# Results written over their own input tile: no result buffers, 14 places for the transposed input, a new order

## The chip, the cores and the metric

One core of one Trainium2 chip. The metric is the device time of one execution in microseconds (us). The kernel before took 220.41 us, the median of three runs (220.10 to 221.13).

## What is computed

Four batches of 12,480 rows x of width 128, 32 inducing rows, and a two-layer block with a hidden width of 2,048, all float32:

```
def mab(q, kv):
    s = scale * (q @ kv.transpose(0, 2, 1))
    s = s - s.max(-1, keepdims=True)
    a = np.exp(s)
    a /= a.sum(-1, keepdims=True) + 1e-09
    return a @ kv
h = mab(I, x)                  # I: the 32 inducing rows, for each batch
x2 = mab(x, h)                 # each row of x attends to the 32 rows of h
hid = x2 @ w_in
return (hid - np.tanh(hid)) @ w_out
```

## The kernel before

A batch b goes through three parts. `first` is mab(I, x): for each of seven tiles s (six of 1,920 rows, the last, "xl", of 960) TensorE makes scores from the transposed tile xT and the inducing rows (L322), VectorE copies them and takes maxima (L348), ScalarE takes exponentials (L398), VectorE transposes them (L402), and TensorE sums them with the tile xn, the same rows in natural layout, over the whole batch into one PSUM bank (L409). xn is loaded from a second copy in memory (L391), or, for the eight tiles listed in `TURNED`, made on the chip from xT with TensorE transposes (L381, L387). `SPLIT` cuts a batch's tiles into two groups with a maximum of each. At the end the matrix hT of the batch is written (L468, L470).

`linear` folds the two-layer block into a 32 x 128 matrix P4 for the batch (L491 to L551). This works while the hidden values are so small, or so alike over the 32 rows, that a bound holds; `bound` evaluates it (L672 to L711), writes `limit`, and a general path that isn't taken here follows.

`second` is mab(x, h) with P4 in place of h, tile by tile (`b_chain`): scores with hT on the same xT tile (L322), VectorE transposes and takes maxima (L594, L596), GpSimd subtracts (L601), ScalarE exponentiates (L603), GpSimd adds two halves into a tile bs (L608), VectorE sums (L611) and inverts (L614), GpSimd scales (L615), VectorE transposes (L618), TensorE multiplies with P4 (L643) into two PSUM tiles of a pool with two places, ScalarE (in the last batch also VectorE) evicts each into half a tile of 960 columns (L649), and SP stores it (L653).

So an xT tile is loaded once and used by `first` and later by `second`. Buffers come from pools whose sizes are in `PLACES`: ten places for xT, five for xn (which also hold the raw weights, L277, while they are converted, L281 to L302), five for the result halves `ot`, ten bs tiles. In the last batch two results share a free xT place instead.

All loads and stores are issued by SP, in one queue. The order on every engine is made when the program is built: each operation has a cost and a priority, mostly a sum of numbers of `ORD`, and `Plan.order` lets each engine start the ready operation with the lowest priority whose buffers are free. Engines then execute in that fixed order, each waiting for what it needs. Into planned gaps of TensorE, as far as `FILL` allows, matmuls without use are put (L734).

Of the kernel before, what the change touches and what calls it, by code (L numbers as in the profile page):

```python
# [20 lines left out]
SEG = 480  # L21
KB = SEG // 32
NT = 4
SG = NQ * SEG
SMALL = 0.0625
SERIES = (1.0 / 3.0, -2.0 / 15.0, 17.0 / 315.0)
ROUND = 2.0 ** -24
FILL = 0.5
PLACES = dict(xT=10, xn=5, s1=1, be=5, bt=3, et=3, ot=5, ps=3, o=2, bs=10, D=1, M4=1, P1=2, P4=2)

ORD = dict(first=(-45, 295, 470, 815), second=(630, 840, 935, 580), fs=15, ss=23, lx=-271, ln=-96, lns=3, turn=61,
           keep=0, q=-129, half=-504, late=51, guard=859, win=-335, wout=-461, lwin=-435.5, lwout=32.5, store=-199,
           base=8)
TURNED = {(0, 0), (0, 1), (0, 2), (0, 4), (1, 5), (2, 2), (2, 5), (3, 3)}

SPLIT = {1: 5, 2: 4, 3: 5}
IN_LAG, OUT_LAG = 3, 1.7
SLACK = 1.0e-3

POLY = (0.333333333, -0.133333309, 0.0539675967, -0.0218625754, 0.00882625035,  # L40
# [24 lines left out]
class Plan:  # L65
# [5 lines left out]
    def add(self, eng, cost, fn, reads=(), writes=(), pri=0.0, lag=0.15, turn=None, other=None):  # L71

        deps = set()
        for x in reads:
            if x.writer:
                deps.add(x.writer)
        for x in writes:
            if x.writer:
                deps.add(x.writer)
            deps.update(x.readers)  # L80
        op = Op(eng, cost, fn, deps, list(dict.fromkeys([*reads, *writes])), pri, lag + (0.1 if eng == "PE" else 0.0))
        op.turn, op.other = turn, other
        for x in reads:
            x.readers.append(op)
        for x in writes:
            x.writer, x.readers = op, []
        for x in op.bufs:
            x.left += 1
        self.ops.append(op)
        return op  # L90
# [90 lines left out]
def fused_kernel(ctx, tc, xT, xn, xl, indT, w_in, w_out, outT):  # L181
    nc = tc.nc
    C, NTOK = xT.shape
    B = xn.shape[0]
# [27 lines left out]

    plan = Plan(PLACES)
    add = plan.add

    def io_buf(tag, shape):
        return Buf(lambda: io.tile(shape, F32, name=tag, bufs=PLACES[tag]), tag)

    def small(name, shape, bufs=2):
        return Buf(lambda: io.tile(shape, F32, name=name, bufs=bufs))  # L220

    def misc():
        return Buf(lambda: ps_m.tile([128, 512], F32, name="ps_m"), "ps")
# [9 lines left out]
    sums_all = small("S_all", [128, B * NSG * KB], 1)  # L233
    bs_tiles = [io.tile([128, KB, m // 2 + 1], F32, name=f"bs_{k}", bufs=1) for k in range(PLACES["bs"])]
    bs_next = itertools.count()
# [83 lines left out]
    def scores(ps, rows, w):  # L319

        for q, row in enumerate(rows):
            nc.tensor.matmul(ps[q * m:(q + 1) * m, :SEG], lhsT=w, rhs=row, start=True, stop=True)  # L322

    def attend(b, pri, s1, group, nbs, sms, at, hacc):
# [9 lines left out]
        for s in group:  # L334
# [3 lines left out]
                out=x.get()[:, :nq * SEG], in_=xT[:, b * N + base:b * N + base + nq * SEG]),  # L338
                writes=[x], pri=pri + s - ORD["lx"], lag=IN_LAG, turn="xT")
            ps = misc()  # L340

            def pe(x=x, ps=ps, nq=nq):
                t = x.get()[:, :nq * SEG].rearrange("c (k q j) -> c k q j", k=KB, j=32)
                scores(ps.get(), [t[:, :, q, :] for q in range(nq)], indT_sb)
            add("PE", 0.96, pe, reads=[x, ind_b, s1], writes=[ps], pri=pri + ORD["fs"] * s)

            def out(ps=ps, s=s, P=nq * m):
                nc.vector.tensor_scalar(out=s1.get()[:P, s, :], in0=ps.get()[:P, :SEG], scalar1=1.0, scalar2=None,  # L348
                                        op0=ALU.mult, op1=ALU.max, accum_out=mxg.get()[:P, s:s + 1])
            add("DVE", 0.68, out, reads=[ps, s1], writes=[s1_part[s], mxg], pri=pri + ORD["fs"] * s)  # L350

        mx, mr, nb = small("mx", [128, 1], 4), small("mr", [1, m], 4), Buf(lambda: nbs.get()[:, at:at + 1])
        ps, ps2 = misc(), misc()
        p = pri + ORD["base"]
        add("DVE", 0.12, lambda: nc.vector.tensor_reduce(out=mx.get(), in_=mxg.get(), axis=AX.X, op=ALU.max),
# [13 lines left out]
        for s in group:  # L369
# [3 lines left out]
            parts = []  # L373
            if (b, s) in TURNED and nq == NQ:
                for k in range(0, KB, NT):
# [3 lines left out]
                    def turn(pt=pt, k=k, n=n, s=s):  # L379
                        for i in range(n):  # L380
                            nc.tensor.transpose(out=pt.get()[:, i * 128:(i + 1) * 128],  # L381
                                                in_=xT_b[b, s].get()[:, (k + i) * 128:(k + i + 1) * 128], identity=ident)
                    add("PE", 0.13 * n, turn, reads=[xT_b[b, s], x, ident_b], writes=[pt], pri=pri + ORD["fs"] * s + ORD["turn"],
                        turn=None if k else "xn")

                    def keep(pt=pt, k=k, n=n, x=x):
                        nc.scalar.copy(out=x.get()[:, k:k + n, :].rearrange("p k c -> p (k c)"), in_=pt.get()[:, :n * 128])  # L387
                    add("ACT", 0.15 + 0.11 * n, keep, reads=[pt, x], writes=[part], pri=pri + ORD["fs"] * s + ORD["keep"])
                    parts.append(part)
# [27 lines left out]
    def first(b, pri):  # L417
        s1 = io_buf("s1", [128, NSG, SEG])
        cut = SPLIT.get(b, 0) if SPLIT.get(b, 0) < NSG else 0
        groups = [range(0, cut), range(cut, NSG)] if cut else [range(NSG)]  # L420
# [201 lines left out]
    def second(b, s, pri):  # L622
        base, nq = SGS[s]
        x = xT_b[b, s]
        n = (b * NSG + s) * KB

        def out(bt, held):
            ots = []
            for h in range(nq // 2):
                if b < B - 1:  # L630
                    ots.append(io_buf("ot", [128, 2 * SEG]))
                else:
                    if h == 0:

                        wide = io_buf("xT", [C, SG])
                    ots.append(Buf(lambda wide=wide, h=h: wide.get()[:, 2 * h * SEG:2 * (h + 1) * SEG]))
            keep = [wide] if b == B - 1 else []
            tiles = [Buf(lambda: ps_o.tile([128, 2, 512], F32, name="o"), "o") for _ in range(nq // 2)]

            def pe(qs):  # L640
                for q in qs:
                    p = slice(q * m, (q + 1) * m)
                    nc.tensor.matmul(tiles[q // 2].get()[:, q % 2, :SEG], lhsT=P4_b[b].get()[p, :], rhs=bt.get()[p, :],  # L643
                                     start=True, stop=True)

            add("PE", 1.05, lambda: pe(range(nq)), reads=[bt, *held, P4_b[b]], writes=tiles, pri=pri)
            for h, (o, ot) in enumerate(zip(tiles, ots)):
                def ev(copy, o=o, ot=ot):
                    copy(out=ot.get().rearrange("p (q n) -> p q n", q=2), in_=o.get()[:, :, :SEG])  # L649
                add("ACT", 0.97, lambda ev=ev: ev(nc.scalar.copy), reads=[o, *keep], writes=[ot], pri=pri,  # L650
                    other=("DVE", 1.14, lambda ev=ev: ev(nc.vector.tensor_copy), pri + 1000) if b == B - 1 else None)
                at = b * N + base + 2 * h * SEG
                add("SP", 1.2, lambda ot=ot, at=at: nc.sync.dma_start(out=outT[:, at:at + 2 * SEG], in_=ot.get()),  # L653
                    reads=[ot, *keep], pri=pri - ORD["store"], lag=OUT_LAG)
        b_chain(b, nq, x, x.get, pri, lambda: sums_all.get()[:, n:n + KB], out, b == B - 1 and s % 2 == 1)


# [71 lines left out]
    for op in ops:  # L729


        if not any(a < op.start < z for a, z in quiet):
            for _ in range(int(FILL * gaps.get(op, 0.0) / 0.25)):
                nc.tensor.matmul(bank[:, 2 * C:2 * C + 128], lhsT=ident, rhs=ident, start=first_fill, stop=True,  # L734
# [105 lines left out]
```

## Time and profile before

| | |
|---|---|
| median of the runs | 220.41 us |
| profiled execution | 221.32 us, span 219.6 us, mean granted TensorE clock 0.911 |
| TensorE, VectorE, ScalarE, GpSimd busy | 178.1, 155.3, 116.8, 97.8 us |
| DMA | 73.03 MB on the data queue, 87.3% of 16 engines' span |
| read and written | 47.46 MB, 25.56 MB |

Busy shares are averages over stretches with different limits; the prediction reads them stretch by stretch. A DMA share near 1 means that all 16 engines had packets to move all the time. A line number is that of the kernel before; in the kernel after, lines from L640 on are eight lower, so that the output matmul is L635, the eviction L641 and the store L645.

### The profile page before, as it was taken

To read this page: it belongs to the slowest core of one execution; us is meant where nothing else is said; L and a number is where in the kernel's file an instruction comes from. 1 tells how busy PE (TensorE), PEld (TensorE's weight loads), DVE (VectorE), ACT (ScalarE), POOL (GpSimd) and SP (SyncE) were. 2 spreads that over 40 slices of the span, in tenths; PEclk is the share of its full clock that TensorE was granted. 3 is DMA by queue.
4 is the path that set the end of the run, shared out by engine and by line. 5 is a ranking of instruction groups with operands and counts; after the bars stand their busy time and mean duration, and the time that the engine had idled before them with its cause. 6 is when DMAs were issued, how large, how long until landed. Compare 5 with 4: busy or idle time off the path is not lost.

```text
span 219.6 us, 5239 instructions
## 1 busy us (share of the span) xinstructions
PE 178.1 (81%) x2015; PEld 92.7 (42%) x2015; DVE 155.3 (71%) x402; ACT 116.8 (53%) x229; POOL 97.8 (45%) x138
## 2 busy tenths in 40 slices
PE   7565589848968999995799985998997999799740
PEld 7542244744432467332226651334454434346310
DVE  5799986543697995667388953496979048888960
ACT  2426356930324999385178961367943836648310
POOL 1135414000299643339454641189334245989600
PEclk9979679999999999999699995799999559889995
DMA  5999998799999899999999999599999924609793
GB/s 170 414 417 357 322 405 323 268 292 344 417 421 417 262 416 363 423 405 427 416 411 323 336 419 420 192 358 421 361 381 353 378 113 179 237 36 372 286 400 125
DMA packets 15472, 73.44 MB, mean 334 GB/s; under 512 B 1872, under 2 KB 1872, under 8 KB 15440
## 3 DMA queue, kind: packets, MB, share of 16 engines
q1 hardware_dynamic: 15440, 73.03, 87.3%
q8 instruction: 18, 0.29, 0.5%
q14 instruction: 14, 0.11, 0.2%
HBM read 47.46 MB, written 25.56 MB: 333 GB/s over the span
## 4 chain that ended last, share of the span: by engine, by line
PE 46%; DMA 25%; DVE 12%; ACT 6%; POOL 4%; issue 2%; SPq 1%; ACTq 0%; POOLq 0%; DVEq 0%
PE ps_m L322 17%; DMA xT<-in_xT 14%; PE o L643 10%; PE bank L409 6%; PE ps_m L381 5%; DMA outT<-ot 4%; DMA xn<-in_xl 4%; DMA xn<-in_w_out 3%; PE ps_m L491 2%; ACT xn L387 2%; DVE xT L649 2%; ACT s L398 2%; DVE xn L292 1%; DVE xn L298 1%; PE ps_m L549 1%
## 5 line engine op out<-in xcount | busy, mean ns | idle before, releaser
L601 POOL TENSOR_TENSOR be<-be,bmx 128x480 f32<-128x480 f32 (+1 forms) x25 | 25.2, 1013 | 49.3 <-DVE bmx L596 42.6
L322 PE MATMUL ps_m<-xT,indT_sb 128*32 128x480 f32 x208 | 32.6, 667 | 17.8 <-DMA xT<-in_xT 11.5
L649 ACT COPY ot<-o 128x960 f32<-128x960 f32 x39 | 36.4, 959 | 14.7 <-DMA outT<-ot 7.9
L643 PE MATMUL o<-bt,P 32*128 32x480 f32 x184 | 31.9, 654 | 3.6 <-ACT ot L649 2.9
L615 POOL TENSOR_TENSOR be<-be,brs 128x480 f32<-128x480 f32 (+1 forms) x25 | 24.8, 995 | 21.6 <-DVE brs L614 15.3
L409 PE MATMUL bank<-xn,et 128*32 128x128 f32 (+1 forms) x840 | 30.9, 280 | 4.3 <-DMA xn<-in_xn 2.9
L348 DVE TENSOR_SCALAR_CACHE_REDUCE s<-ps_m 128x480 f32<-128x480 f32 (+1 forms) x28 | 18.2, 650 | 20.4 <-PE ps_m L322 20.4
L409 PEld LDWEIGHTS bank<-xn,et 128*32 128x32 f32 (+1 forms) x840 | 23.8, 111 | 14.5 <-issue 5.9
L322 PE MATMUL ps_m<-xT,hT 128*32 128x480 f32 x208 | 28.0, 604 | 0.2 <-ACT D L507 0.2
L387 ACT COPY xn<-ps_m 128x512 f32<-128x512 f32 (+1 forms) x32 | 17.3, 556 | 11.6 <-PE ps_m L381 11.5
L608 POOL TENSOR_TENSOR bs<-be 128x240 f32<-128x240 f32 (+1 forms) x25 | 17.9, 718 | 10.5 <-ACT be L603 10.4
L734 PE MATMUL bank<-ident 128*128 128x128 f32 x110 | 20.2, 328 | 1.9 <-POOL ident masks.py:199 1.4
L402 DVE STREAM_TRANSPOSE et<-s 128x480 f32<-128x480 f32 (+1 forms) x28 | 18.4, 659 | 3.8 <-ACT s L398 3.8
L594 DVE STREAM_TRANSPOSE be<-ps_m 128x480 f32<-128x480 f32 (+1 forms) x25 | 16.5, 661 | 5.7 <-PE ps_m L322 5.7
L734 PEld LDWEIGHTS bank<-ident 128*128 128x128 f32 x110 | 17.6, 236 | 6.8 <-issue 4.5
L381 PE MATMUL ps_m<-ident,xT 128*128 128x128 f32 x120 | 19.5, 300 | 0.7 <-ACT xn L387 0.5
L398 ACT ACTIVATE s<-s,nb 128x480 f32<-128x480 f32 (+1 forms) x28 | 19.4, 696 | 0.7 <-DVE nb L367 0.5
L381 PEld LDWEIGHTS ps_m<-ident,xT 128*128 128x128 f32 x120 | 14.2, 152 | 10.5 <-issue 3.0
L618 DVE STREAM_TRANSPOSE bt<-be 128x480 f32<-128x480 f32 (+1 forms) x25 | 16.6, 664 | 2.3 <-POOL be L615 2.1
L603 ACT ACTIVATE be<-be 128x480 f32<-128x480 f32 (+1 forms) x25 | 14.9, 604 | 3.9 <-POOL be L601 3.9
L322 PEld LDWEIGHTS ps_m<-xT,indT_sb 128*32 128x32 f32 x208 | 5.8, 117 | 26.0 <-issue 10.9
L596 DVE TENSOR_REDUCE bmx<-be 128x15 f32<-128x480 f32 (+1 forms) x25 | 15.7, 633 | 0.1
(126 smaller groups left out, 226.8 us busy)
## 6 DMA issues: line engine op xcount, KB each, us to landing
xT<-in_xT SPq DMA_DIRECT2D x24, 960.0 KB, 9.3
outT<-ot SPq DMA_DIRECT2D x39, 480.0 KB, 8.6
xn<-in_xn SPq DMA_DIRECT2D x16, 960.0 KB, 10.2
outT<-xT SPq DMA_DIRECT2D x13, 480.0 KB, 3.1
xn<-in_w_in SPq DMA_DIRECT2D x4, 512.0 KB, 5.4
xn<-in_w_out SPq DMA_DIRECT2D x4, 512.0 KB, 6.0
xT<-in_xT SPq DMA_DIRECT2D x4, 480.0 KB, 10.4
xn<-in_xl SPq DMA_DIRECT2D x4, 480.0 KB, 8.1
```

The source lines that it names most:

```text
L322: nc.tensor.matmul(ps[q * m:(q + 1) * m, :SEG], lhsT=w, rhs=row, start=True, stop=True)
L348: nc.vector.tensor_scalar(out=s1.get()[:P, s, :], in0=ps.get()[:P, :SEG], scalar1=1.0, scalar2=None, op0=ALU.mult, op1=ALU.max, accum_out= ...
L381: nc.tensor.transpose(out=pt.get()[:, i * 128:(i + 1) * 128], in_=xT_b[b, s].get()[:, (k + i) * 128:(k + i + 1) * 128], identity=ident)
L387: nc.scalar.copy(out=x.get()[:, k:k + n, :].rearrange("p k c -> p (k c)"), in_=pt.get()[:, :n * 128])
L398: nc.scalar.activation(out=sl, in_=sl, func=AF.Exp, scale=SC, bias=nb.get()[:P], accum_out=sums.get()[:P, s:s + 1])
L402: add("DVE", 0.66, lambda et=et, s=s, P=P: nc.vector.transpose(out=et.get()[:P].rearrange("p k i -> p (k i)"), in_=s1.get()[:P, s, :]), re ...
L409: nc.tensor.matmul(hacc.get()[q * m:(q + 1) * m, :], lhsT=et.get()[:P, k, :], rhs=x.get()[:P, k, :], start=(s == group[0] and k < NQ), sto ...
L601: add("POOL", 1.02, lambda: nc.gpsimd.tensor_tensor(out=be.get()[:P], in0=be.get()[:P], in1=wide(bmx.get()[:P]), op=ALU.subtract), reads=[ ...
L615: add("POOL", 1.02, lambda: nc.gpsimd.tensor_tensor(out=be.get()[:P], in0=be.get()[:P], in1=wide(brs.get()[:P]), op=ALU.mult), reads=[brs] ...
L643: nc.tensor.matmul(tiles[q // 2].get()[:, q % 2, :SEG], lhsT=P4_b[b].get()[p, :], rhs=bt.get()[p, :], start=True, stop=True)
L649: copy(out=ot.get().rearrange("p (q n) -> p q n", q=2), in_=o.get()[:, :, :SEG])
L734: nc.tensor.matmul(bank[:, 2 * C:2 * C + 128], lhsT=ident, rhs=ident, start=first_fill, stop=True, skip_group_check=not first_fill)
```

## The change

A step of `second` no longer takes result buffers. ScalarE evicts the result over the step's own xT tile, and the store reads it from there, so that the place of an xT tile is free only when its store has landed.

```
-PLACES = dict(xT=10, xn=5, s1=1, be=5, bt=3, et=3, ot=5, ps=3, o=2, bs=10, D=1, M4=1, P1=2, P4=2)
+FILL = 0.6                                           # 0.5 before
+PLACES = dict(xT=14, xn=4, s1=1, be=5, bt=4, et=4, ps=3, o=2, bs=1, D=1, M4=1, P1=2, P4=2)
-ORD = dict(first=(-45, 295, 470, 815), second=(630, 840, 935, 580), fs=15, ss=23, lx=-271, ln=-96, lns=3, turn=61,
+ORD = dict(first=(-65, 385, 570, 780), second=(780, 1015, 1000, 615), fs=20, ss=36, lx=-289, ln=2, lns=24, turn=52,
...
-TURNED = {(0, 0), (0, 1), (0, 2), (0, 4), (1, 5), (2, 2), (2, 5), (3, 3)}
-SPLIT = {1: 5, 2: 4, 3: 5}
-IN_LAG, OUT_LAG = 3, 1.7
+TURNED = {(0, 0), (0, 1), (0, 4), (0, 5), (1, 1), (2, 4), (2, 5), (3, 0)}
+SPLIT = {0: 4, 1: 4, 2: 3, 3: 5}
+IN_LAG, OUT_LAG = 2, 1.7

         def out(bt, held):
-            ots = []
-            for h in range(nq // 2):
-                if b < B - 1:
-                    ots.append(io_buf("ot", [128, 2 * SEG]))
-                else:
-                    if h == 0:
-                        wide = io_buf("xT", [C, SG])
-                    ots.append(Buf(lambda wide=wide, h=h: wide.get()[:, 2 * h * SEG:2 * (h + 1) * SEG]))
-            keep = [wide] if b == B - 1 else []
+            ots = [Buf(lambda h=h: x.get()[:, 2 * h * SEG:2 * (h + 1) * SEG]) for h in range(nq // 2)]
...
-                add("ACT", 0.97, lambda ev=ev: ev(nc.scalar.copy), reads=[o, *keep], writes=[ot], pri=pri,
+                add("ACT", 0.97, lambda ev=ev: ev(nc.scalar.copy), reads=[o, x], writes=[ot], pri=pri,
...
-                    reads=[ot, *keep], pri=pri - ORD["store"], lag=OUT_LAG)
+                    reads=[ot, x], pri=pri - ORD["store"], lag=OUT_LAG)
```

Most of it is seen in the order only. The first place is SP's queue around the first stores. Before (a tile's name carries a number that tells its copies apart; ot is a result half, in_xT, in_xn and outT are in memory):

```order
L337 DMA xT_722<-in_xT 128x960
L337 DMA xT_738<-in_xT 128x1920
L337 DMA xT_769<-in_xT 128x1920
L653 DMA outT<-ot_758 128x960
L653 DMA outT<-ot_771 128x960
L337 DMA xT_837<-in_xT 128x1920
L653 DMA outT<-ot_812 128x960
L653 DMA outT<-ot_841 128x960
L391 DMA xn_912<-in_xl 64x1920
```

And now, in the same queue:

```order
L391 DMA xn_901<-in_xn 128x1920
L391 DMA xn_937<-in_xn 128x1920
L391 DMA xn_978<-in_xn 128x1920
L645 DMA outT<-xT_126 128x960 x2
L645 DMA outT<-xT_133 128x960
L337 DMA xT_1048<-in_xT 128x1920
L645 DMA outT<-xT_133 128x960
L645 DMA outT<-xT_165 128x960 x2
L337 DMA xT_1129<-in_xT 128x1920
L337 DMA xT_1170<-in_xT 128x1920
L645 DMA outT<-xT_193 128x960 x2
```

The first store is the first half-tile of batch 0 in both. Ahead of it now stand the loads of all 14 xT tiles of batches 0 and 1 and of eleven whole xn tiles, four of them (xn_848 to xn_978) for batch 2; behind it stores and loads alternate, and a load of xT_1048 needs the place of xT_126, two rows above it, xT_1129 that of xT_133, and so on.

The second place is the end of the loads in SP's queue. Before:

```order
L653 DMA outT<-ot_1891 128x960
L391 DMA xn_1967<-in_xn 128x1920
L391 DMA xn_2004<-in_xl 64x1920
L653 DMA outT<-ot_1727 128x960
L653 DMA outT<-ot_1748 128x960
L653 DMA outT<-ot_2002 128x960
```

Now:

```order
L337 DMA xT_1878<-in_xT 128x1920
L645 DMA outT<-xT_1048 128x960 x2
L337 DMA xT_1934<-in_xT 128x960
L645 DMA outT<-xT_1129 128x960 x2
L391 DMA xn_1977<-in_xn 128x1920
L391 DMA xn_2011<-in_xn 128x1920
L391 DMA xn_2059<-in_xl 64x1920
L645 DMA outT<-xT_1170 128x960 x2
```

The last load is the xl tile of the last batch in both. 25 half-tile stores stood ahead of it and 27 behind; now it is 30 and 22.

The third place is TensorE's queue around the last sum over the last batch, which reads that xl tile. Before:

```order
L449 MATMUL ps_m_2085<-sm_1997,fold_71 128x1 x2
L409 MATMUL bank_92<-xn_1967,et_2067 32x128 x15
L643 MATMUL o_2115<-bt_2030,P4_1820 128x480 x2
L643 MATMUL o_2118<-bt_2030,P4_1820 128x480 x2
L409 MATMUL bank_92<-xn_2004,et_2076 32x128 x15
L734 MATMUL bank_92<-ident_70 128x128
L468 MATMUL ps_m_2158<-fold_71,P1_2154 128x32
L643 MATMUL o_2164<-bt_2148,P4_1820 128x480 x2
```

Now:

```order
L409 MATMUL bank_83<-xn_2011,et_2106 32x128 x15
L449 MATMUL ps_m_2135<-sm_2037,fold_71 128x1 x2
L409 MATMUL bank_83<-xn_2059,et_2128 32x128 x15
L635 MATMUL o_2159<-bt_2033,P4_1842 128x480 x2
L635 MATMUL o_2162<-bt_2033,P4_1842 128x480 x2
L468 MATMUL ps_m_2167<-fold_71,P1_2165 128x32
L726 MATMUL bank_83<-ident_70 128x128
```

The output matmul (o) of the batch before moved from ahead of the last sum to behind it.

More of the change, by code (lines that the diff above doesn't have):

```diff
@@ L27 @@
 ROUND = 2.0 ** -24
-FILL = 0.5
-PLACES = dict(xT=10, xn=5, s1=1, be=5, bt=3, et=3, ot=5, ps=3, o=2, bs=10, D=1, M4=1, P1=2, P4=2)
-ORD = dict(first=(-45, 295, 470, 815), second=(630, 840, 935, 580), fs=15, ss=23, lx=-271, ln=-96, lns=3, turn=61,
-           keep=0, q=-129, half=-504, late=51, guard=859, win=-335, wout=-461, lwin=-435.5, lwout=32.5, store=-199,
-           base=8)
-TURNED = {(0, 0), (0, 1), (0, 2), (0, 4), (1, 5), (2, 2), (2, 5), (3, 3)}
-SPLIT = {1: 5, 2: 4, 3: 5}
-IN_LAG, OUT_LAG = 3, 1.7
+FILL = 0.6
+PLACES = dict(xT=14, xn=4, s1=1, be=5, bt=4, et=4, ps=3, o=2, bs=1, D=1, M4=1, P1=2, P4=2)
+ORD = dict(first=(-65, 385, 570, 780), second=(780, 1015, 1000, 615), fs=20, ss=36, lx=-289, ln=2, lns=24, turn=52,
+           keep=-40, q=-192, half=-353, late=207, guard=912, win=-554, wout=-388, lwin=-482.5, lwout=50.5, store=-49,
+           base=39)
+TURNED = {(0, 0), (0, 1), (0, 4), (0, 5), (1, 1), (2, 4), (2, 5), (3, 0)}
+SPLIT = {0: 4, 1: 4, 2: 3, 3: 5}
+IN_LAG, OUT_LAG = 2, 1.7
 SLACK = 1.0e-3
```

## The prediction

> **What bounds the kernel now.** I read the page first, then the stretches of the span, then the chain of waits backwards from the end, and last the sync engine's own waits.
>
> ```profile
> span 219.6 us, 5239 instructions
> PE 178.1 (81%) x2015; PEld 92.7 (42%) x2015; DVE 155.3 (71%) x402; ACT 116.8 (53%) x229; POOL 97.8 (45%) x138
> DMA  5999998799999899999999999599999924609793
> q1 hardware_dynamic: 15440, 73.03, 87.3%
> HBM read 47.46 MB, written 25.56 MB: 333 GB/s over the span
> ```
>
> No engine is full over the whole span, but the DMA row stands at 9 for most of the first 32 slices (176 us). Then it drops: the loads are over and the stores wait for results. So there are two problems, one behind the other: when does the last load land, and how long is the tail after it? The stretches show both (busy time of PE, PEld, DVE, ACT, POOL; then granted clock, DMA share, GB/s).
>
> ```profile
> 0.00:72.00 72.00, 52.77 (x558) 32.06 (x558) 52.40 (x132) 30.23 (x63) 24.13 (x35) 0.93 0.94 351
> 72.00:130.00 58.00, 54.31 (x772) 28.21 (x768) 43.28 (x127) 41.56 (x84) 28.70 (x40) 0.97 1.00 381
> 130.00:160.00 30.00, 25.92 (x261) 10.26 (x257) 20.75 (x56) 16.36 (x35) 14.49 (x24) 0.89 0.92 356
> 160.00:177.40 17.40, 14.35 (x198) 8.27 (x194) 9.54 (x26) 10.78 (x17) 6.81 (x8) 0.80 0.97 364
> 177.40:194.60 17.20, 15.64 (x124) 5.88 (x124) 12.86 (x27) 8.30 (x18) 12.87 (x22) 0.81 0.38 147
> 194.60:213.00 18.40, 15.14 (x122) 7.98 (x122) 16.46 (x41) 9.53 (x14) 10.77 (x13) 1.00 0.74 294
> 213.00:219.60 6.60, 0.00 (x0) 0.00 (x0) 0.00 (x0) 0.00 (x0) 0.00 (x0) 0.63 0.45 166
> ```
>
> Up to 177.4 the transfers are the bound (share 0.92 to 1.00); from there to 213.0 it is the chain of work of the last batch, with VectorE busy 29.3 of 35.6 us. The seam is 177.4, when the last batch's column matrix (hT, line 470) is ready. The chain of waits (start, us, what) tells why it is ready only then:
>
> ```profile
> 159.63 0.47 SPq L391
> ...
> 160.16 9.40 DMA outT<-ot
> ...
> 169.63 0.97 ACT ot L649
> ...
> 170.64 3.12 PE o L643 x8
> 173.76 1.89 PE bank L409 x30
> ...
> 175.74 0.36 DVE P L461
> ...
> 176.94 0.27 PE ps_m L468 x2
> ```
>
> The last load, the xl tile, is issued at 159.63. A store issued behind it lands at 169.56; only then may ScalarE evict into that result buffer, only then is a PSUM place free for an output matmul on TensorE, and the last sum over the batch (L409) stands behind that matmul in TensorE's queue. The tile itself had long landed; the two timelines and the landing time of that one load:
>
> ```profile
> 169.63 0.96 ACT L649 COPY ot<-o 128x960 f32<-128x960 f32 x1 [3.71 <-DMA outT<-ot]
> 177.25 0.19 DVE L470 COPY hT<-ps_m 128x32 f32<-128x32 f32 x1 [0.55 <-PE ps_m L468]
> DMA to landing us min/median/max: 8.7/8.7/8.7
> ```
>
> 159.63 + 8.7 = 168.3, but hT is there at 177.44: 9.1 us. In the first batch, where nothing stood between, the same steps took 2.7 us (landing at 51.83; its end is at 54.31 with the 0.19 us copy behind it):
>
> ```profile
> 43.76 8.07 DMA xn<-in_xl
> ...
> 51.96 1.07 PE bank L409 x30
> ...
> 54.31 0.94 PE ps_m L322 x8
> ```
>
> So 6.4 us of the 9.1 hang on the result buffers.
>
> **The change part by part.**
>
> *Result buffers gone.* ScalarE writes over the step's x, whose readers (scores, transposes) are done. No eviction waits for a store any more, and the output matmul that stood ahead of the last sum now stands behind it; the 6.4 us before the tail go. Nothing is late next at that place but the landing of the xl tile.
>
> *When that tile lands.* The queue in the new order carries 28.8 MB ahead of the first store (8 weight pieces of 0.524 MB, 14 x tiles of 0.98 MB, two of them half as large, or 12.8 MB, and 11.8 MB of xn and xl) against 26.3 MB before: 14 places take all x of two batches, so no load waits there for a score. Ahead of the last load it carries all 47.46 MB of reads and 30 half-tile stores of 0.49 MB (before: 25), 62.2 MB (before: 59.7). At the rates of full share, 351/0.94 = 373 GB/s at the start and 381 later: 1.2 us of start + 28.8/0.373 = 77.2 + 33.4/0.381 = 87.7, together 166.1 us without a gap.
>
> *Gaps.* This is the disputed term. A load of x may now be issued only when the store out of the same place has landed, 14 times, and while SP waits for that, everything behind it in the queue waits too. Before, it waited for matmuls and evictions; the rows (total, times, longest), and the stores of the tail with an almost empty queue:
>
> ```profile
> SPq L653 <- ACT ot L649: 49.8, 22, 7.2
> SPq L337 <- PE ps_m L322: 27.1, 14, 7.4
> SPq L391 <- PE bank L409: 17.7, 12, 6.0
> outT<-xT SPq DMA_DIRECT2D x13, 480.0 KB, 3.1
> DMA to landing us min/median/max: 2.6/3.1/5.4
> ```
>
> A store of 0.49 MB moves in 1.3 us at 381 GB/s, so about 1.8 us of its 3.1 are start and completion in which the engines could move other data, if any is queued. With an issue (0.47 us in the chain's first row) that is 2.2 us per reuse. In the new order a load or one to four half-tile stores stand between a store and the load that needs its place: 1.3 us of cover at three of the 14, 2.6 us or more at the others. Bounds: 0 (a shortfall that other queued work hides) to 14 x 2.2 = 31 us (no cover at all). Three times 0.9 short is 2.7; I nearly double it for evictions that come late and take 5 us. It is near the covered end, as the stretch from 72 to 130 ran at share 1.00 although SP waited often there too. The tile lands at 171.1, hT is ready at 171.1 + 2.7 = 173.8: 3.6 us earlier than 177.4.
>
> The Trainium skill's page "DMA: Bandwidth & Descriptors", section "Anatomy of one DMA", speaks against this edit: a DMA costs about 2.0 us fixed, most of it the receipt of the last written byte, heaviest where the target is HBM, as for these stores. Its formula gives 3.1 us for 0.49 MB, and the row's 3.1 agrees (the page fits it for another issuing path). With 2.0 us uncovered at each of the 14 waits its sum would be 28 us instead of my 5, and that is the second rival below.
>
> *xn from 5 places to 4.* The last three loads (two tiles and xl) each wait for a sum over an earlier tile; before it was two. Their place in the queue is behind the stores anyway. Cost 0 by the count above; it reappears as a rival.
>
> *Weights spread out, another first order.* The four pieces of w_out are loaded between x tiles; the same conversions, on the same engines, all before the first linear step. Batch 0 is now summed in two groups, about ten short instructions more; eight tiles are transposed on the chip as before, other ones, so the bytes stay; one more place each for et and bt can only take waits away. Cost 0, cover: VectorE has 52.4 of 72 us busy in the first stretch; without that cover the first store would come later and DMA would idle after 28.8 MB are through.
>
> *The tail.* From hT to the end it took 219.6 - 177.4 = 42.2 us. Rows of VectorE in it:
>
> ```profile
> 177.88 0.68 DVE L618 STREAM_TRANSPOSE bt<-be 128x480 f32<-128x480 f32 x1 [0.44 <-POOL be L615]
> 178.53 0.41 DVE L611 TENSOR_REDUCE S_all<-bs 64x15 f32<-64x255 f32 x1
> 178.97 0.24 DVE L614 RECIPROCAL brs<-S_all 64x15 f32<-64x15 f32 x1
> ...
> 184.53 0.66 DVE L618 STREAM_TRANSPOSE bt<-be 64x480 f32<-64x480 f32 x1
> ...
> 208.97 0.37 DVE L705 TENSOR_REDUCE low<-ps_m 1x2 f32<-1x256 f32 x1
> ...
> 210.15 0.14 DVE L711 TENSOR_SCALAR limit<-low 1x1 f32<-1x1 f32 x1
> ...
> 211.76 1.16 DVE L649 COPY xT<-o 128x960 f32<-128x960 f32 x1 [0.37 <-PE o L643]
> ```
>
> The first four belong to the batch before and now stand ahead of hT: 2.0 us off. VectorE evicts four results instead of five: 1.16 off. The limit's steps (208.97 to 210.29, 1.3 us) move behind the last eviction, beside its store: 1.3 off. Against it: one bs tile for ten, so each half-add on GpSimd (L608) waits for VectorE's sum of the step before, 0 to 7 x 0.41 = 2.9 us, I take 1.2; and more filler matmuls (71 instead of 55 in the order, three or four of them in the tail), 0 to 1.2, I take 0.6, since TensorE waits for VectorE there. Net -4.5 + 1.8 = -2.7; the rest of the tail is the same work.
>
> *Sum.* 173.8 + 42.2 - 2.7 = 213.3 us of span against 219.6: 6.3 less. The profiled execution took 221.32 us, 0.9 above the median of the runs, 220.41; I take the difference from the median: 214.1 us.
>
> **The rivals.**
>
> 1. *The places come free too late* (slower). Mechanism: SP stands at a load until a store's completion, and the queue behind it is too short, at each of the 14 reuses between the first store and the last load. For: the 2.2 us of the fixed part; SP issues in order, so a late eviction also holds the loads. Against: the cover by stores in between. With half of the 31 us uncovered, 15.5 instead of 5: 224.6 us; at none covered 240. It decides from 11.3 us of gaps, or 0.8 us per reuse.
>
> 2. *The wait moves* (no change). The last three xn loads hang on four places: each needs a sum, the sum an exponential, that the maximum over five x tiles, whose loads need stores. If these run one behind the other and the xl tile lands near 174.5 instead of 171.1, and the tail saves nothing (one bs tile eats it), it is 219.4 us of span, 220.2. For: 17.7 us of waits for xn places today with five; against: the tiles are small against the stores queued ahead.
>
> 3. *Better than summed.* No gap at all (166.1), and the tail loses its whole 4.5 us: 206.5 us of span, 207.3. For: SP no longer waits 49.8 us for evictions that themselves wait. Against: 0.92 in the stretch from 130 to 160, where loads wait for matmuls.
>
> **How the numbers follow.** Forecast 0.53, rival 3 0.05, rival 2 0.14, rival 1 0.28. Faster by over 0.5% (under 219.3; that much is about what a measurement here tells from nothing): 0.58; within: 0.14; slower: 0.28. The forecast's own range is 209 to 219: gaps 0 to 10 us. With rival 1 up to about 14 us over it and rival 3 at the low end, 207 to 227 leaves out some 0.17.
>
> **What would show it.** In the changed profile: a DMA row without a dip before the first store and the first 28.8 MB through by about 78 us; no eviction that waits for a store; the last L409 starting within 0.3 us of the xl tile's landing, hT near 174; about 39 us from there to the end. Wrong if SP's waits for stores' landings, followed by a DMA share under 0.9 between 78 and 165, add up to over 11 us, or if hT comes after 178.

## The result: slower by 9.4%, and the profile after

| | before | after |
|---|---|---|
| median of the runs | 220.25 us (218.99 to 221.13) | 241.46 us (239.99 to 247.75) |
| ratio | | 1.0944, 95% interval 1.0855 to 1.1032 |
| profiled execution, span | 221.32 us, 219.6 us | 241.12 us, 239.3 us |
| hT of the last batch ready | 177.4 us | 198.3 us |
| from there to the end | 42.2 us | 41.0 us |

The forecast was 214.1 us with a range to 227; the time lies outside it, at the price of rival 1 with no cover at all (240). Some executions of any kernel take a few per cent longer: ratios here and below compare the others alone, and where too few of them remained there is none; medians, ranges and differences are of all runs.

The page of the kernel after: its span, its engines, its DMA rows.

```profile
span 239.3 us, 5310 instructions
PE 191.5 (80%) x2058; PEld 100.8 (42%) x2058; DVE 152.5 (64%) x403; ACT 118.4 (49%) x232; POOL 96.0 (40%) x138
DMA  6999999699899988999989799998889994238891
GB/s 189 417 420 405 371 395 383 242 305 334 306 322 236 414 340 245 335 328 334 317 292 290 204 360 336 361 371 287 313 309 354 303 344 180 105 144 329 330 387 41
HBM read 47.46 MB, written 25.56 MB: 305 GB/s over the span
```

The bytes are those of before. The DMA row still shows 8 and 9 in most slices, but from slice 15 to 33 (a slice is 6.0 us; the first store is issued in slice 14) the GB/s row stands between 204 and 371. By stretches (busy time of PE, PEld, DVE, ACT, POOL; granted clock, DMA share, GB/s), cut at the first store, the last load, close to hT and at the end of the engines' work:

```profile
0.00:79.70 79.70, 66.09 (x809) 41.72 (x811) 56.60 (x157) 37.43 (x83) 20.81 (x32) 0.89 0.92 335
79.70:187.40 107.70, 85.02 (x859) 38.65 (x851) 64.51 (x167) 55.61 (x108) 52.15 (x74) 0.90 0.91 319
187.40:197.80 10.40, 8.83 (x153) 5.36 (x152) 4.91 (x19) 4.78 (x10) 2.01 (x2) 0.87 0.94 324
197.80:232.90 35.10, 31.59 (x248) 15.08 (x247) 26.48 (x62) 20.57 (x34) 21.03 (x31) 0.94 0.62 245
```

In the second stretch no engine is full (TensorE comes closest, 85.0 of 107.7 us) and the transfers run at 319 GB/s, against 381 in the stretch from 72 to 130 before. SP's waits name what is new, and the chain of waits shows it as a loop (start, us, what):

```profile
SPq L337 <- DMA outT<-xT: 53.7, 15, 7.7
SPq L645 <- ACT xT L641: 45.1, 28, 7.9
SPq L391 <- PE bank L409: 20.9, 10, 4.2
```

```profile
81.21 8.14 DMA outT<-xT
...
89.42 0.34 SPq L337
...
89.86 7.33 DMA outT<-xT
...
97.20 6.40 DMA xT<-in_xT
...
112.43 9.64 DMA outT<-xT
...
122.15 7.18 DMA xT<-in_xT
```

A store lands at 89.35, and the load for its place is issued at 89.42. The next store is issued behind it, lands at 97.19, and 0.01 us later its place is loaded, which takes until 103.60; and so on to the end of the loads, with scores, outputs and evictions in between. SP's own timeline shows the queue standing in between (xn is the last load before the first store; "x3" is three issues in a row):

```profile
79.75 4.29 SPq L645 DMA_DIRECT2D outT<-xT  x3
89.42 0.34 SPq L337 DMA_DIRECT2D xT<-in_xT  x1
89.86 1.83 SPq L645 DMA_DIRECT2D outT<-xT  x3
97.20 2.70 SPq L337 DMA_DIRECT2D xT<-in_xT  x2
99.95 2.84 SPq L645 DMA_DIRECT2D outT<-xT  x4
109.25 2.61 SPq L337 DMA_DIRECT2D xT<-in_xT  x2
```

From 84.0 to 89.4, 91.7 to 97.2 and 102.8 to 109.3 SP issues nothing. What that does to the transfers shows around the first landing (columns as in the stretches):

```profile
84.00:88.00 4.00, 4.00 (x38) 1.92 (x34) 3.26 (x10) 2.93 (x6) 4.00 (x6) 1.00 1.00 406
88.00:90.00 2.00, 2.00 (x18) 0.45 (x10) 2.00 (x5) 1.61 (x6) 1.66 (x6) 1.00 0.38 148
90.00:92.00 2.00, 2.00 (x20) 1.23 (x16) 1.75 (x5) 1.47 (x3) 1.92 (x4) 1.00 0.84 134
92.00:94.00 2.00, 0.97 (x31) 0.78 (x33) 2.00 (x5) 1.52 (x3) 1.84 (x6) 1.00 0.98 292
```

The queue runs thin before the store lands (148 GB/s), and the load issued then takes until 94 to bring the rate back. Against 406 GB/s these six us move 1.29 MB too little, 3.2 us' worth. At the end, the part that the prediction had right, the timeline around the last sum:

```profile
187.37 0.47 SPq L391 DMA_DIRECT2D xn<-in_xl  x1
...
194.38 1.24 PE L409 MATMUL bank<-xn,et 64*32 64x128 f32 x30
...
195.55 1.98 PE L635 MATMUL o<-bt,P 32*128 32x480 f32 x8
...
197.47 0.64 PE L468 MATMUL ps_m<-fold,P 128*128 128x32 f32 x2
...
198.14 0.19 DVE L470 COPY hT<-ps_m 128x32 f32<-128x32 f32 x1 [2.05 <-PE ps_m L468]
```

In the chain that load takes 6.97 us, so it lands at 194.34; the sum starts 0.04 us later, with no eviction and no output matmul ahead of it. From landing to hT it is 4.0 us, against 9.1 before: what came late is the landing.

### The profile page after: what moved, and what is told of

Read it like the earlier page. It is cut to its first block, busy times and chain, and to the rows that moved or that the text cites. A ratio compares the mean times of both kernels' runs of the same rounds, so it can differ in the third digit from the quotient of the medians.

```text
span 239.3 us, 5310 instructions
## 1 busy us (share of the span) xinstructions
PE 191.5 (80%) x2058; PEld 100.8 (42%) x2058; DVE 152.5 (64%) x403; ACT 118.4 (49%) x232; POOL 96.0 (40%) x138
## 4 chain that ended last, share of the span: by engine, by line
DMA 50%; PE 23%; DVE 7%; POOL 7%; ACT 5%; issue 3%; SPq 1%; POOLq 0%; DVEq 0%
DMA xT<-in_xT 22%; DMA outT<-xT 16%; PE ps_m L322 8%; DMA xn<-in_xn 7%; PE o L635 5%; PE bank L409 4%; ACT xT L641 3%; DMA xn<-in_xl 3%; DMA xn<-in_w_in 2%; PE ps_m L491 2%; PE ps_m L381 2%; POOL bs L608 1%; POOL be L601 1%; POOL xn L615 1%; DVE xT L641 1%
## 5 line engine op out<-in xcount | busy, mean ns | idle before, releaser
L641 ACT COPY xT<-o 128x960 f32<-128x960 f32 x48 | 44.8, 960 | 32.0 <-PE o L635 32.0
L322 PE MATMUL ps_m<-xT,indT_sb 128*32 128x480 f32 x208 | 35.3, 712 | 24.2 <-DMA xT<-in_xT 23.9
L601 POOL TENSOR_TENSOR be<-be,bmx 128x480 f32<-128x480 f32 (+1 forms) x25 | 25.7, 1030 | 38.0 <-DVE bmx L596 37.9
L409 PE MATMUL bank<-xn,et 128*32 128x128 f32 (+1 forms) x840 | 33.0, 286 | 8.1 <-DMA xn<-in_xn 5.1
L635 PE MATMUL o<-bt,P 32*128 32x480 f32 x184 | 31.8, 679 | 0.4 <-DVE bt L618 0.2
L409 PEld LDWEIGHTS bank<-xn,et 128*32 128x32 f32 (+1 forms) x840 | 25.1, 113 | 15.5 <-DMA xn<-in_xn 4.2
L322 PE MATMUL ps_m<-xT,hT 128*32 128x480 f32 x208 | 29.4, 606 | 0.2 <-DVE xn L594 0.2
L726 PE MATMUL bank<-ident 128*128 128x128 f32 x142 | 25.6, 323 | 1.4 <-POOL ident masks.py:199 1.4
L726 PEld LDWEIGHTS bank<-ident 128*128 128x128 f32 x142 | 21.4, 225 | 10.9 <-issue 8.2
L381 PE MATMUL ps_m<-ident,xT 128*128 128x128 f32 x120 | 20.2, 309 | 0.3 <-ACT xn L387 0.2
L381 PEld LDWEIGHTS ps_m<-ident,xT 128*128 128x128 f32 x120 | 14.9, 157 | 9.5 <-issue 4.0
L302 POOL TENSOR_TENSOR wout_sb<-wout_sb,xn 128x512 f32<-128x512 f32 x4 | 5.5, 1374 | 32.3 <-DVE rs L453 17.8
```

The source lines that it names most:

```text
L409: nc.tensor.matmul(hacc.get()[q * m:(q + 1) * m, :], lhsT=et.get()[:P, k, :], rhs=x.get()[:P, k, :], start=(s == group[0] and k < NQ), sto ...
L601: add("POOL", 1.02, lambda: nc.gpsimd.tensor_tensor(out=be.get()[:P], in0=be.get()[:P], in1=wide(bmx.get()[:P]), op=ALU.subtract), reads=[ ...
```

## The experiments

Theory A: the loss is the loop through a store's landing; each load that needs the place of a stored tile holds SP until then, and the transfers run thin. Its rivals: the new numbers (order, places), one store held behind another in SP's queue, a loop closed by TensorE, and transfers that are slow rather than missing.

**Structure and numbers apart.** `inplace_old` is the code of after with the numbers of before (12 places for xT); `buffers_new` is the code of before with the numbers of after.

```diff
 # inplace_old: after's code
+PLACES = dict(xT=12, xn=5, s1=1, be=5, bt=3, et=3, ps=3, o=2, bs=10, ...)   # ORD, TURNED, SPLIT, lags of before
 # buffers_new: before's code
+PLACES = dict(xT=12, xn=4, s1=1, be=5, bt=4, et=4, ot=4, ps=3, o=2, bs=1, ...)   # ORD, TURNED, SPLIT, lags of after
```

> The edit in the structure alone: results over their own x tile, but all other numbers (order, splits, xn=5, bs=10, bt, et) of the kernel before; the memory of the five result halves goes to xT, 12 places. Theory A (a place that is free only when a store has landed makes loads, scores and stores run in lock-step, whatever the order): 232 to 245 us, and SP's waits of loads for stores' landings above 30 us in all. Theory B (the new order and the smaller pools are what costs; the place itself is harmless): 216 to 224 us, those waits under 15 us.

> The other half: all the numbers of the kernel after (order, splits, xn=4, bs=1, bt=4, et=4, filler), but results in buffers of their own again, as before; four halves for them, paid with two xT places (12). Theory A: no load waits for a store's landing, so most of the loss is gone, 216 to 226 us. Theory B: the new order costs with buffers too, 232 to 245 us.

Measured: in place with the old numbers 260.70 us, ratio 1.184 (1.174 to 1.194), over theory A's own range, with 58.4 us of loads that wait for stores' landings; the new numbers with result halves 224.40 us, ratio 1.0225 (1.015 to 1.030). So writing in place, two more xT places included, costs 40 us with the one set of numbers and 17 us with the other; the new numbers with halves (12 places for xT, four halves) cost 4. The loss belongs to the structure; the new numbers had softened it.

**The landing taken out of the loop.** `store_constant` is after, in the same order on every engine, but a store reads a constant tile of the same size, so that the results are left out and a load waits for the eviction alone. The edit takes a second wait away, which its expectation does not name: a store no longer waits for its own eviction, SP's second row in after (45.1 us).

```diff
-in_=ot.get()),
+in_=win_sb[:, :2 * SEG]),
```

> The kernel after in the same order on every engine, with one wait taken away: each store still moves its 128x960 floats to the output, but out of a constant tile (the weights), so that a place is free once the result has been evicted, not once its store has landed. What is stored is not the result. Theory A (the landing of the stores in the loop is what costs): 217 to 227 us. Theory C (the place is simply held too long, from the first scores to the eviction, and the landing adds little): 233 to 241 us.

Measured: 219.26 us, ratio to before 1.0025 (0.996 to 1.009); 22.2 us below after (20 by the two ratios). The stretch from first store to last load (columns as above):

```profile
78.40:165.10 86.70, 75.31 (x859) 35.76 (x851) 64.71 (x168) 55.80 (x108) 52.28 (x74) 1.00 1.01 395
```

The same 859 matmuls and about the same bytes (395 x 86.7 = 34.2 MB; after: 319 x 107.7 = 34.4 MB) take 21.0 us less, and the longest wait of a load of x is 3.7 us, for an eviction (second row below). Nearly the whole loss goes with the two waits. Most of it is the landing, as theory A has it: `stores_own_queue`, below, also frees SP of the wait for evictions but keeps the landing, and takes 238.68 us, 19.4 more than this kernel.

The run also shows that my sum without gaps was 6.5 us short: the last load lands at 172.6, not at 166.1. Most of that is lost before the first store. Up to 78.4 us the transfers ran at 340 GB/s and moved 26.7 MB, where the sum has 28.8. The wait that rival 2 named is there too: SP waits 32.8 us for places of xn (20.9 in after), and before the last three loads its timeline stands from 153.3 to 161.2. The transfers show that only at its end (407 GB/s from 159 to 160, 181 from 161 to 162). Waits, then timeline:

```profile
SPq L391 <- PE bank L409: 32.8, 13, 7.1
...
SPq L337 <- ACT xT L641: 11.4, 5, 3.7
```

```profile
151.75 1.51 SPq L645 DMA_DIRECT2D outT<-win_sb  x2
161.21 2.21 SPq L391 DMA_DIRECT2D xn<-in_xn  x2
165.09 0.47 SPq L391 DMA_DIRECT2D xn<-in_xl  x1
```

**Half of the reuses.** `constant_half` does the same, to both waits, for the stores of batch 0 alone; seven of the fourteen reusing loads still wait for a landing.

```diff
+in_=ot.get() if b else win_sb[:, :2 * SEG]),
```

> After, in the same order, but the stores of batch 0 alone read a constant tile instead of x (their results are left out), so that only the seven loads of batch 3, which take the places of batch 1, wait for a store's landing. Theory A (each reuse costs by itself, 22 us for fourteen): 228 to 233 us, hT of the last batch near 187. Rival (one closed loop, in which the reuses left set the pace, or in which time won early is lost again in waits later): 236 to 242 us.

Measured: 232.92 us (229.75 to 235.64), ratio 1.0525 (1.042 to 1.063), hT at 189.1. Half of the waits gone, 8.5 of the 22.2 us gone: the cost comes reuse by reuse. That it is a little less than half fits the order, where the reuses stand in nine groups (one or two loads behind a run of stores) and five of the nine are left; one run does not prove this.

**Idle or slow?** `spare_loads` puts a load of 0.246 MB into a spare tile ahead of each reusing load; `spare_heads` only ahead of the nine groups.

```diff
+if b > 1:                                         # spare_heads: and s in (0, 1, 3, 5, 6)[:b + 2]
+    nc.sync.dma_start(out=spare, in_=xT[:, base:base + SEG])
 nc.sync.dma_start(out=x.get()[:, :nq * SEG], ...)
```

> After's order, but ahead of each of the 14 loads of x that reuse a place SP issues one more load, half as large as a half-tile store (0.246 MB), into a spare tile that nobody reads: 3.4 MB more to move, 9.2 us at 373 GB/s, and 14 more issues. Theory A (the engines stand idle while SP waits for a store's landing; the loss of about 24 us is idle time): the extra loads lie in the idle time, 240 to 245 us, 0 to 4 us over after's 241.5, and the stretch from the first store to the last load shows a DMA share at least 0.03 higher than after's 0.91. Rival (the loop is slow because transfers are, so that more bytes lengthen it): 248 to 252 us.

Measured: 252.47 us, 11.0 over after, just above the rival's range and far from theory A's. SP's waits show why this does not count for the rival: where two reuses follow each other, the second extra load waits for the first one's landing into the one spare tile:

```profile
SPq L340 <- DMA spare<-in_xT: 15.9, 8, 2.9
```

So this run had added eight more waits for a landing, and was inconclusive on its question.

> As the kernel with spare loads (252.5 us, in which eight extra loads waited 15.9 us for the extra load before them), but with an extra load only ahead of a reuse that stands behind a store: 9 instead of 14, far enough apart that none waits for the spare tile. 2.2 MB more to move, 5.9 us at 373 GB/s. Theory A (the engines are idle while SP waits for a landing): no waits at the extra loads, 240.5 to 244 us, at most 2.5 us over after's 241.5 (nine issues of 0.34 us, part of them in the wait). Rival (the transfers themselves are slow, so that more bytes lengthen the loop): 246.5 to 250 us.

Measured: 242.41 us (239.65 to 245.40), ratio 1.110 (1.102 to 1.119); 0.95 us over after, where 2.2 MB more take 5.9 us at 373 GB/s. No extra load waits for the spare tile. SP's wait for landings is still there, and hT comes when it came in after:

```profile
SPq L341 <- DMA outT<-xT: 48.4, 14, 7.8
```

```profile
198.05 0.19 DVE L474 COPY hT<-ps_m 128x32 f32<-128x32 f32 x1 [0.91 <-PE ps_m L472]
```

The extra bytes lay in time in which the DMA engines could have moved more. The transfers are not at a limit of their rate; too little is queued for them.

**Other ways to close the loop.** `stores_own_queue` issues the stores from ScalarE; `resident_scores` lets the first scores of batches 2 and 3 read a resident tile instead of the loaded one (those scores are left out).

```diff
 # stores_own_queue
-nc.sync.dma_start(out=outT[...], in_=ot.get())
+nc.scalar.dma_start(out=outT[...], in_=ot.get())
 # resident_scores
+t = (x.get() if b < 2 else win_sb)[:, :nq * SEG]...
```

> The kernel after in the same order, but the stores of results are issued from ScalarE's queue, right behind the eviction, so that SP no longer holds a store behind a load that waits for a landing, nor a load behind a store that waits for its eviction. If the loss is SP's head-of-line waiting (28 waits for evictions, 15 for landings): 222 to 232 us. If it is the latency around the loop of landing, load, score, output matmul, eviction, store: 235 to 243 us, since each link stays. If the issuing itself burdens ScalarE, at most 52 x 0.3 = 16 us on an engine with 118 of 239 us busy, it shows there.

> The kernel after in the same order, with the other link of the loop cut: in batches 2 and 3 the first scores read the weights' tile in place of the x tile just loaded, so that TensorE does not wait there for a load (transposes and second scores still read x). The results of these batches are others. Theory A with the loop closed through TensorE's fixed order (an output matmul queued behind a score whose load waits for an earlier store): 220 to 230 us. If loads come late whatever TensorE does, because SP alone is the chain (store, landing, load, store): 234 to 242 us.

Measured: 238.68 us (234.78 to 241.12) and 239.50 us, ratio 1.0935 (1.082 to 1.105). With the stores issued from ScalarE the loads wait 82.6 us for landings, and the last load is issued at 187.27, against 187.37 in after. One of the four runs lies 5 us below all of after's, so up to that much may come from stores and loads that stand behind each other in one queue; most of the loss does not. Nor does it come from the first scores that wait for a load; the later reads of the loaded tile stayed, and were not tested. The Trainium skill's page "DMA: Bandwidth & Descriptors", section "Issuing engines are not separate DMA queues", says that another issuing engine saves only its sequencer's time. These runs agree in so far as at most a few us were saved.

**Telling the plan.** The order is made with an allowance of 1.7 us from a store's issue to its landing. `plan_late_stores` is after with 6.5; `inout7` raises the allowance for loads too; `before_late_stores` does it in before.

```diff
-IN_LAG, OUT_LAG = 2, 1.7
+IN_LAG, OUT_LAG = 2, 6.5       # inout7: 7, 6.5; before_late_stores: 3, 6.5
```

> The kernel after with one number changed: the planner believes that a store takes 6.5 us from the end of its transfer to the landing (the median from issue to landing in the trace of after) instead of 1.7. It then orders more work between a store and the load that takes its place. Theory A, and the loss comes from an order that sends TensorE to a score before the load can be there: 225 to 235 us, TensorE's waits for xT loads well under the 23.9 us of after. Theory B, or if no order can hide the landings: 238 us or more.

> After, with both allowances of the plan raised: a landing of a store 6.5 instead of 1.7, of a load 7 instead of 2, so that the order is made for places that come free late and tiles that come late. Theory A: the waits for landings get covered by other rows of the queue, as with the store's allowance alone (228.0 us), 219 to 229 us. Rival (fourteen reuses cost the same wherever they stand): 236 to 242 us.

> The kernel before, its planner told 6.5 us for a store's landing instead of 1.7. If the planner's belief matters only where places wait for stores all the time: within 2 us of before. If it is too short for the result halves as well (7.9 us of evictions that wait for a store in the trace of before): 3 to 6 us less than before, 214 to 217 us.

Measured: 227.98 us (223.44 to 231.35); 225.31 us, ratio 1.025 (1.015 to 1.034); 225.46 us, ratio 1.024 (1.010 to 1.038). An order that knows of the landing gives back 13 to 16 of the 22 us: it puts other rows of the queue between a store and its place's load, and SP's waits for landings fall from 53.7 us to 19.9 and 32.2. The third is a miss: in before, where no load waits for a store, the truer number makes a worse order, 5 us slower. Why was not followed up.

**One bs tile or three.** `bs3_same_order` is after with three bs tiles, in after's order.

> The kernel after in the same order on every engine, but with three bs tiles used in turn, so that GpSimd's half-add does not wait for VectorE's sum of the step before. The prediction put 1.2 us on this (0 to 2.9), nearly all in the tail: 1 to 3 us less than after, 238.5 to 240.5 us. If the one tile also slows the middle (9.0 us of GpSimd's waits for that sum in the trace of after): 5 to 9 us less.

Measured: 241.96 us (237.37 to 245.33), inconclusive as a time. In its profiled execution (238.81 us) the tail took 39.3 us instead of 41.0, but not through the bs tiles: from L534, a step of `linear`, to the last step of the limit both kernels take 25.7 us. The 1.7 us lie ahead of it, where TensorE's granted clock was 0.65 in after (198.3 to 203.6) and 1.00 here.

**The gain without the loop.** Was the 6.4 us of the eviction real? `hybrid_old` is before with results in place only in the last ten x tiles, whose places nobody reloads; `hybrid_new` is the same on `buffers_new`.

```diff
-if b < B - 1:
+if b * NSG + s < B * NSG - PLACES["xT"]:
     ots.append(io_buf("ot", [128, 2 * SEG]))
 else:
-    ... wide = io_buf("xT", [C, SG]) ...
+    ots.append(Buf(lambda h=h: x.get()[:, 2 * h * SEG:2 * (h + 1) * SEG]))
```

> Before, with results written over x only where no load follows into the place (the last ten x tiles, of 28); all others keep the five result halves. No load waits for a store's landing, as in before, and fewer evictions wait for a result half at the seam. Theory A (the loss is all in load after store, the gain promised for the eviction is real): no waits of a load of x for a store, the 6.4 us that the column matrix hT of the last batch waited behind an eviction shrink, 214 to 219 us. Rival B (at the seam something else, the bytes ahead of the last load, decides): 219 to 222 us. Rival C (the rearranged order costs more than the freed halves bring): over 222 us.

> The kernel with the new numbers, four result halves and twelve places for x (224.4 us), with results written over x only where no load follows into the place (the last twelve of 28 tiles). Theory A: as in the other hybrid the evictions of the end need no result half, 216 to 223 us, below 224.4. Rival (the halves were not what bound this order): 223 to 227 us.

Measured: 220.42 us, ratio 0.999 (0.994 to 1.004), and 231.49 us, ratio 1.048 (1.039 to 1.057), a miss by theory A's number (the order came out otherwise, and its cause stays open). In the first an eviction of batch 2 still waited for the store of a result half, as the chain shows (161.64 to 170.81). So two more runs give it halves, in the memory of nine bs tiles: `before_ot7` and `hybrid_ot7`. The order was made anew for both.

```diff
-ot=5, ps=3, o=2, bs=10,
+ot=7, ps=3, o=2, bs=1,
```

> Before, with seven result halves instead of five, in the memory of nine of the ten bs tiles; nothing in place. Theory A (the wait of an eviction for a store at the seam, 6.4 us, is the part of the change's reasoning that was right, and two more halves take most of it without closing a loop through the landing of a store): hT of the last batch at 172 to 176 instead of 177.4, 215 to 219 us. Rival (at the seam the next wait takes its place, or one bs tile gives it back): 219.5 to 223 us.

> The hybrid of before (results in place in the last ten x tiles only; 220.4 us, in which an eviction at the seam still waited for the store of a result half from 161.6 to 170.8), with seven result halves instead of five, in the memory of nine of the ten bs tiles. Theory A: that wait goes, hT of the last batch at 172 to 176 instead of 178.5, 214 to 218 us. Rival (as for the kernel with seven halves alone): 219 to 223 us.

Measured: 215.84 us (213.03 to 220.25), ratio 0.978 (0.970 to 0.987), and 214.51 us (211.54 to 218.49), ratio 0.978 (0.972 to 0.985). Both beat before, and after by 26 to 27 us. ScalarE's groups of evictions into halves, before and then with seven halves (instructions | busy, mean ns | idle ahead of them and what ended it), and hT with seven halves:

```profile
L649 ACT COPY ot<-o 128x960 f32<-128x960 f32 x39 | 36.4, 959 | 14.7 <-DMA outT<-ot 7.9 <-PE o L643 4.2 <-issue 1.7
```

```profile
L649 ACT COPY ot<-o 128x960 f32<-128x960 f32 x39 | 36.3, 957 | 8.8 <-PE o L643 4.0 <-issue 3.2 <-ACT s L398 0.9
```

```profile
170.10 0.19 DVE L470 COPY hT<-ps_m 128x32 f32<-128x32 f32 x1 [0.72 <-PE ps_m L468]
```

Of the 7.9 us for stores 0.2 remain, and hT comes at 170.3 instead of 177.4. In the hybrid it comes at 167.8; the stretch up to its last load and its hT:

```profile
72.00:157.20 85.20, 78.22 (x1017) 37.64 (x1017) 63.46 (x177) 57.98 (x118) 42.46 (x62) 0.96 1.00 382
```

```profile
167.61 0.19 DVE L470 COPY hT<-ps_m 128x32 f32<-128x32 f32 x1 [0.72 <-PE ps_m L468]
```

The two ratios cannot be told apart: what both kernels have is free halves at the seam. Since the orders differ from that of before too, it is the eviction's row and hT, rather than the time alone, that tie the gain to the halves.

## Why the prediction was wrong

**Result buffers gone: right.** The wait it named was on the path and worth nearly what it said. With seven halves hT comes 7.1 us earlier: 5.5 because it takes 3.6 us from the last load's landing instead of 9.1, and 1.6 because that load lands earlier (166.7). I took 6.4 for the first part alone. In after no eviction waits for a store.

**Up to the first store: some 6 us too early.** I took 28.8 MB as through by 78.4 us (1.2 + 28.8/0.373). The first store was issued near that, at 79.75, but by then 26.7 MB had moved (335 GB/s x 79.7); at the 406 GB/s that followed, the rest was through near 85. The 373 GB/s came from dividing 351 by the share of 0.94, as if the new order left no gaps there. It did (share 0.92): the GB/s row dips to 242 in slice 8, behind 9.2 us for which SP stood for a place of xn that a piece of w_out needed. I had priced the weights and the four xn places at 0.

**Gaps: the step that failed.** I priced a reuse at 2.2 us, the store's start and completion (1.8) and an issue, set 1.3 to 2.6 us of queued stores against it, and took 5 us for all fourteen. With the two waits of `store_constant` away the kernel is 22.2 us faster and the last load lands 21.7 us earlier, so the term was more than four times too small. The tile landed 23.2 us later than I said, at 194.3: 16.7 by this term, 6.5 by the sum without gaps. What the term left out is the load's own start and completion. SP holds the load back until the store has landed; by then the queue has run thin (148 GB/s), and the load begins from almost nothing (134 GB/s from 90 to 92 us). The row of x loads between the first store and the last load in after:

```profile
DMA to landing us min/median/max: 4.7/6.3/8.1
```

Even the fastest took 4.7 us, 2.1 more than its 0.98 MB need at 381 GB/s. As an estimate from these rows a turnaround is then 1.8 + 0.34 (the issue) + 2.1 = 4.24 us; fourteen are 59, less the cover that I counted, 3 x 1.3 + 11 x 2.6 = 32.5, leaves 27 us, against 22.2 measured. No run takes the load's start out by itself, so this split is not shown. I had also placed the term near its covered end because the stretch from 72 to 130 ran at share 1.00 while SP waited. But there SP waited for matmuls and evictions with loads still in flight; here the wait is for the landing of a store near the end of the queue, so that little is left in flight when it ends. A wait of SP is covered only by transfers that were issued before it began.

**What the prediction quoted against itself.** Its sentence on the section "Anatomy of one DMA" of the Trainium skill's page "DMA: Bandwidth & Descriptors" gave, as an estimate, 28 us for a fixed 2.0 us uncovered at fourteen waits (it calls that the second rival; it belongs to the first). The measured 22.2 us lie near that, in part by luck: by the estimate above a turnaround has two such parts, the store's and the load's, partly covered, rather than one that is bare.

**The sign of a failure.** I said it would show as SP's waits for landings followed by a DMA share under 0.9. SP's waits did (53.7 us), hT came after 178, but the share was 0.91 in the stretch that lost 21 us. The GB/s column had it. The row without a dip before the first store did not come either (slice 8).

**From the landing to hT, and the tail: off by 1.3 and 1.5 us.** I took 2.7 us from the landing, as in the first batch; it was 4.0, since an output matmul (1.98 us, L635) stands between the last sum and L468, as the order had shown, and since TensorE's granted clock was 0.61 there (194.3 to 198.3). The tail took 41.0 us against 39.5. My 1.2 us for the single bs tile are not its cause: GpSimd's half-adds waited 9.0 us for VectorE's sums, but none of it after hT. The granted clock goes with both: in `store_constant`, the same order at 1.00 in both places, the two took 3.0 and 38.5 us, and with three bs tiles, at 1.00 behind hT, the tail took 39.3. From hT to L534 it is 8.8 us in after and 7.1 in each of the others. Why the clock differed was not followed up.

**Rivals.** Rival 1 held, with its place and mechanism, at 0.28; only its price with no cover came near. Rival 2's wait is seen once the landings are out of the way, as a small term. That `store_constant` comes out level with before (219.26 us), and not faster, is owed more to the transfers ahead of the first store (26.7 instead of 28.8 MB by 78.4 us).

## What to carry to other kernels

A buffer that a store reads is not free when its data are in flight but when they have landed, and a load into it then starts with little else in flight: price such a reuse as store completion plus issue plus the load's own start (4.2 us here, by estimate), not as one of them, and subtract only transfers that are already issued when the queue's engine begins to wait. Result buffers pay for themselves by keeping the landing of stores out of the way of loads; look at which wait ends last and give that place one or two more buffers, before giving them up. When a planner sets the order, a duration that it underrates (here 1.7 us for landings of 6 us and more) can do no harm, as in before, and cost a great deal once loads hang on it, as in after.

## What the runs showed of the hardware

The busy share of the DMA engines is no measure of bytes: 34.4 MB took 0.91 x 107.7 = 98 us of busy share in after and 34.2 MB 1.01 x 86.7 = 88 us in `store_constant`. With a thin queue packets take longer: behind the first landing of after a share of 0.84 moved 134 GB/s. So a stretch with gaps can still show 0.91, and the rate (319 against 395 GB/s) tells it. With the stores issued from another engine most of the loss stayed (238.68 against 241.46 us): the landing itself, more than the queue in which it is waited for, sets the pace. And TensorE's granted clock was not the same at the same place of the same order (0.65 behind hT in after, 1.00 in `store_constant`), and the steps from hT to L534 took 8.8 and 7.1 us.
